# When one weight half is loaded for GpSimd, and which PSUM bank the 256-token groups use, in a fused attention and expert-routing kernel

## The chip, the cores and the metric

The kernel runs on one core of a Trainium2 chip. The metric is the time on the device for one execution, in microseconds (us). Lower is better. Matrix products run on TensorE (PE in the profile), elementwise work on VectorE (DVE), ScalarE (ACT) and GpSimd (POOL). Transfers are issued in order by a queue of SyncE (SP) and, for some, by GpSimd. SBUF is the on-chip memory of 128 partitions; PSUM holds the results of products, in banks of 512 float32 per partition; DRAM lies outside.

## What is computed

The reference first computes an attention without softmax, then a layer of eight experts with Sinkhorn weights. All is float32.

```
# attention: batch 4, heads 4, 1088 tokens, head size 32, r = 8
phi(x): a = S1 x, b = S2 x; outer product of a and b, 64 features
kv  = sum over tokens of phi(k) v^T;   z = sum over tokens of phi(k)
out = (phi(q) kv) / (phi(q) z + 1e-6)
x   = out as (4352 tokens, 128)

# experts: D = 128, E = 8, F = 1024
P = exp(x w_gate - max)
8 times: P /= rows' sums; P /= columns' sums; P *= N / E
out = sum over e of P[:, e] * (relu(x w1[e]) w2[e])
```

## The kernel before

**Stages.** The work runs in three overlapping stages. The attention takes the batches 0 to 3 one after the other (`attention(b)`), then `routing()` computes the logits and eight Sinkhorn rounds. The tokens' features end in `xT` (128 features by 4352 tokens). Since TensorE would often wait during these two stages, `fill(n)` lets it do expert products there that need no routing weights: `steps()` is a generator of such work, one step per call, and the numbers that `attention` and `routing` yield say how many steps' worth go between two of their parts. After that comes the long weighted stage (from about 213 us on), where the other experts' products are computed with tokens already multiplied by their routing weight.

**The groups.** `steps()` walks through 13 groups in the order of the list `groups` (line 672). Each has an expert, a first token and a number n of tokens. Groups 0, 1, 3, 5, 6 and 8 belong to expert 0. Groups 2, 4, 7, 9, 10, 11 and 12 are "SMALL": the first 256 tokens with the experts 1, 2, 4, 3, 5, 6 and 7. A small group has two blocks of four steps. An expert-0 group has four blocks, and works on two sets of n tokens at once. In each step TensorE computes one hidden chunk (`first`, line 787), ScalarE applies Relu to it (line 789), and TensorE issues second products that belong to hidden chunks of eight steps earlier (`LAG = 8`, `into`, line 851).

**Two kinds of second products.** The small groups and group 0 add up plain products (`eight`) in one or two banks of PSUM. The other groups use Strassen-like combinations with seven products instead of eight (`seven`). VectorE forms the differences that they need (line 802), and the products add up in four banks: bank 0 holds p1 and p6, bank 1 p2 and p4, bank 2 p3 and p5, bank 3 p7. In each block they are issued in this order.

**Emptying the banks.** When the last product of a bank is done, `into` calls `part`. For a small group that is one ScalarE copy to `kept_small` (line 699). For a group with seven products it is `part_of_seven`: three copies for bank 0 (lines 723, 724, 726), one for bank 1 (730), three for bank 2 (734 to 736) and two for bank 3 (739, 740). ScalarE works in order, and its Relus stand between these copies. The banks are tiles of the pool `mps` with the tags `s0` to `s3`, one buffer each: whoever takes a tag next waits until the copies out of it are done. In `into` a small group's tag is its expert's number modulo 4. So the groups 2, 4, 7, 9 and 10 use the banks 1, 2, 0, 3 and 1. Groups 11 and 12 are put off and use other lines (866).

**Weights for the small groups.** Expert 1's weights lie in `wb`, in columns 3F to 5F (F = 1024). Expert 2's take the same place: `small_load(2, ...)` is called within `steps()` at the third block of group 3 and issues two transfers on SyncE's queue (lines 1007 and 1010, 512 KB each). Experts 3 to 7 are loaded in `routing()` by `small_weights()`; expert 4's go to `xfs[0]` (called `xf0`).

**Packing on GpSimd.** For the weighted stage, weights are turned into the combinations that the seven products need. Three of these halves are formed by GpSimd at the end of the attention: (4, 0) and (5, 0), the first-layer weights of the experts 4 and 5, and (5, 1), the second-layer weights of expert 5. `bench_load(n, where, e, i)` loads a raw half on SyncE's queue: line 230 for a first-layer half, four transfers of 128 KB, and line 235 for a second-layer half. `bench_pack(n)` has GpSimd do four subtractions or additions (line 201) and then store the result to DRAM (line 247, `packed`). Bench 0 holds (4, 0) and lies in `xf0`; bench 1 holds (5, 1) and lies in two tiles named `qx`; bench 2 holds (5, 0) and lies in `xf0` again. The store of a first-layer half reads a part of the raw half as well, so the next load into `xf0` has to wait until that store is done.

**What orders the queues.** TensorE, VectorE and ScalarE run in the written order during these stages (`manual_schedule`). SyncE's and GpSimd's transfers and GpSimd's arithmetic keep program order too. An instruction at the head of a queue that waits holds up all behind it. In `attention(2)` the order is: the raw halves of bench 0 and bench 1 are asked for; later `take_over(2, ...)` has GpSimd store the finished attention output (`xd`, line 510) and bring it back turned into `xT` (four transfers of line 512), then GpSimd packs bench 0, and bench 2 is loaded. In `attention(3)` `take_over` is issued in two parts: columns 0 to 192 by GpSimd, columns 192 to 288 by SyncE. `logits` (line 520) reads `xT` of all batches. At the start of `routing()` GpSimd packs bench 2 and then bench 1; then the pools of the attention are closed and `first_weights` and `raw_second` load the weights for the weighted stage (`w1f`, `w2r`).

Of the kernel before, what the change touches and what calls it, by code (L numbers as in the profile page):

```python
# [53 lines left out]
def kernel(  # L54
# [38 lines left out]
    xfs = [big.tile([P, 8, 256], F32, name="xf0"),  # L93
           *(wb[:, 2 * F * i:2 * F * (i + 1)].rearrange("p (c n) -> p c n", c=8) for i in range(2))]
# [154 lines left out]
    def raw_half(e, i, raw):  # L249
        if i:  # L250
            load_w2(e, raw.rearrange("p (f d) -> p f d", d=DM))
        else:
            load_w1_halves(e, raw)
# [6 lines left out]
    def halves_in(t):  # L260
        t = t.rearrange("p a n -> p (a n)")[:, 0:32 * H2]
        return t[:, 0:16 * H2], t[:, 16 * H2:], t
# [6 lines left out]
    def bench_load(n, where, e, i):  # L269
        benches[n] = e, i, *where()  # L270
        raw_half(e, i, benches[n][2])
# [47 lines left out]
    def transpose_q(b, lo=0, hi=S):  # L319
        to = kT if b == 1 else qT  # L320
        nc.vector.transpose(out=to[:, lo:hi], in_=loaded["q", b].rearrange("p a d -> p (a d)")[:, lo:hi])
# [38 lines left out]
    def keys_sums(b):  # L360

        kp, vx = products[b], v_slots[b % 2]
        pv = bank()[:, 0:128].rearrange("p (i c d) -> p i c d", i=2, c=2)

        slots = [slice(h, H + 1, H - h) for h in range(H)]

        for t in range(NT + 1):
            n = P if t < NT else 64
            for h in range(H):
                i, s = divmod(h, 2)  # L370
                nc.tensor.matmul(pv[64 * s:64 * (s + 1), i], kp[0:n, H * t + h].rearrange("p i j -> p (i j)"),  # L371
                                 vx[0:n, slots[h], t, :], start=(t == 0 and i == 0), stop=(t == NT and i == 1),
                                 tile_position=(0, 64 * s))
        sums_of[b] = pv
# [3 lines left out]
    def keys_kept(b):  # L378
        pv = sums_of.pop(b)
        for s in range(2):  # L380
            sl = slice(64 * s, 64 * (s + 1))
            if b:
                x, y = kvs[b % 2][sl, :, s, :], pv[sl].rearrange("p i c d -> p i (c d)")[:, :, 0:D + 1]
            else:
                x, y = kvz[sl, :, :, s, :], pv[sl].rearrange("p i c d -> p c i d")
            nc.scalar.copy(x, y)
# [88 lines left out]
    def times(b, c):  # L475
        ph = third(phs[b % 2], c)
        nc.vector.tensor_tensor(ph, ph, third(rb, c), op=Alu.mult)
# [53 lines left out]
    def attention(b):  # L531


        follows = b + 1 < B
        keys_sums(b)
        times(b, 0)
        yield 2.2 if b == 1 else 2
        keys_kept(b)
        times(b, 1)
        tops(b, 0)  # L540
        if b == 1:
            transpose_q(2)
        yield 1.4
        times(b, 2)
        over(b, 0)
        tops(b, 1)
        if b == 1:
            queries_ab(2)
            repeat_a(2)
        if follows:  # L550
            repeat_b(b + 1)
        if b == 2:
            bench_load(0, lambda: halves_in(xfs[0]), 4, 0)
            bench_load(1, halves_in_two, 5, 1)
        yield 1.4
        over(b, 1)
        if b + 1 == B:
            take_over(b, 0, 192, nc.gpsimd)
        yield 1.4
        tops(b, 2)  # L560
        if follows:
            transpose_k(b + 1)
        if b + 2 < B:
            load_k(b + 2)
            load_v(b + 2)
        yield 1.4
        over(b, 2)
        if b + 1 < B:
            take_over(b, 0, W9, nc.gpsimd)
            if b == 2:  # L570
                bench_pack(0)
                bench_load(2, lambda: halves_in(xfs[0]), 5, 0)
        else:
            take_over(b, 192, W9, nc.sync)
        if follows:
            yield 0.7
            keys_ab(b + 1)
            yield 0.7
            if b == 1:
                transpose_q(3)  # L580
            keys_products(b + 1, 0)
            yield 1.4
            keys_products(b + 1, 1)
            if b == 1:
                queries_ab(3)
                repeat_a(3)
            yield 1.4
            keys_products(b + 1, 2)
            yield 1.4
# [10 lines left out]

    def routing():

        for n in (2, 1):
            bench_pack(n)
        early.close()
        pools.append(ctx.enter_context(tc.tile_pool(name="late", bufs=2)))
        for i in range(3):
            first_weights(i)
            raw_second(i)
        small_weights()  # L610
        yield 5
        for c in range(len(chunks)):
            logits(c)
        yield 1
        for c in range(len(chunks)):
            logits_turned()
        lg = lgp[:, :, 0:E]
        mx = sk.tile([P, 1], F32, tag="mx", name="mx")
        nc.vector.tensor_reduce(out=mx, in_=lg, axis=AX.XY, op=Alu.max)
        yield 3  # L620
        pm = bank()[:, 0:P]
        for s in range(2):
            nc.tensor.matmul(pm[64 * s:64 * (s + 1)], mx.to_broadcast([P, 64]), ident, start=True, stop=True,
                             tile_position=(0, 64 * s))
        nc.vector.reduce_max(mx, pm, axis=AX.X)
        nc.vector.tensor_scalar(mx, mx, -1.0, 64 * math.log(2.0), op0=Alu.mult, op1=Alu.add)
        pw = p2s[0]
        nc.scalar.activation(out=pw[:, :, 0:E], in_=lg, func=Act.Exp, bias=mx[:, 0:1])

        step = 1.5 * 2.0 ** (23 - 149 + 64)  # L630
        nc.vector.tensor_scalar(pw[:, :, 0:E], pw[:, :, 0:E], step, step, op0=Alu.add, op1=Alu.subtract)
        for it in range(ITERS):
            rs = sk.tile([P, SA], F32, tag="rs", name="rs")
            nc.vector.reduce_sum(rs, pw, axis=AX.X)
            nc.vector.reciprocal(rs, rs)
            p1 = p1s[it % 2]
            nc.vector.scalar_tensor_tensor(p1[:, 0:SA], rs.unsqueeze(2).to_broadcast([P, SA, E]), UP,
                                           pw[:, :, 0:E], op0=Alu.mult, op1=Alu.mult)
            cs = sk.tile([P, E], F32, tag="cs", name="cs")
            nc.vector.reduce_sum(cs, p1.rearrange("p g e -> p e g"), axis=AX.X)  # L640
            yield 4.25
            pc = bank()[:, 0:E]
            for s in range(2):
                nc.tensor.matmul(pc[64 * s:64 * (s + 1)], ones[:, 0:64], cs, start=True, stop=True,
                                 tile_position=(0, 64 * s))
            cr = sk.tile([P, E], F32, tag="cr", name="cr")
            nc.vector.reciprocal(cr, pc)
            last = it == ITERS - 1
            pw = lgp if last else p2s[(it + 1) % 2]
            nc.vector.scalar_tensor_tensor(pw[:, :, 0:E], cr.unsqueeze(1).to_broadcast([P, SA, E]),  # L650
                                           float(N) / E * (1.0 if last else UP), p1[:, 0:SA],
                                           op0=Alu.mult, op1=Alu.mult)

        nc.vector.transpose(out=lgT.rearrange("p a s -> p (a s)"), in_=lgp.rearrange("p a e -> p (a e)"))
        for b in range(B):
            nc.sync.dma_start(out=pT[:, b * S:(b + 1) * S],
                                                  in_=lgT[32 * b:32 * b + E].rearrange("p a s -> p (a s)"))
# [16 lines left out]
    SMALL = {g for g, group in enumerate(groups) if group[2][0]}  # L674
    DIRECT = {0, *SMALL}
# [3 lines left out]
    items = [(g, e) for g, group in enumerate(groups) for e in group[2]]  # L679
# [160 lines left out]
    def into(g, w, x, i, s):  # L840

        n = groups[g][1]
        if g not in sums:
            banks = (items[g][1] % 4,) if g in SMALL else range(2) if g in DIRECT else range(4)
            sums[g] = [mps.tile([P, 512], F32, tag=f"s{i % 4}", name="s")[:, 0:n] for i in banks]
            done[g] = {}

        seen = done[g]
        c = seen[i, s] = seen.get((i, s), 0) + 1
        per = FO if g in DIRECT else FO // 4 if i == 3 else FO // 2  # L850
        nc.tensor.matmul(sums[g][i][H2 * s:H2 * (s + 1)], w, x, start=c == 1, stop=c == per, tile_position=(0, H2 * s))  # L851
        if c == per:
            seen[i] = seen.get(i, 0) + 1
            if seen[i] == 2:
                part(g, i)
# [585 lines left out]
```

## Time and profile before

| quantity | us |
|---|---|
| median of 3 runs | 917.51 |
| lowest and highest of the 3 | 917.27, 919.56 |
| the profiled execution | 920.07 |
| its span, from the first to the last instruction | 918.1 |

The profile comes from one execution. TensorE's clock is granted by a throttle; its mean over the span was 0.996 of full speed. In lines of the profile, `L787` is line 787 of the kernel, `a<-xT,wb` is what an instruction writes and reads by the program's names, and `x4` a count. `[8.13 <-DMA wb<-...]` says how long the engine was idle before, and what ended the wait. Times are in us from the start of the span. Matmuls are pipelined, so a matmul's end in the records can overlap the next one's start; each float32 product appears as two records, and a pair of products, one for each half of the columns, as four.

### The profile page before, as it was taken

Reading aid. Unit: us, or ns where it says so; the run is one execution under the profiler, and the core shown is the slowest. Engines: PE = TensorE matmul, PEld = TensorE weight load, DVE = VectorE, ACT = ScalarE, POOL = GpSimd, SP = SyncE. Lnnn points to the kernel's source line nnn. Section 1 sums busy time; section 2 is a strip of 40 time slices with the busy share of each in tenths; the row PEclk is TensorE's granted clock in tenths of the full one; section 3 lists DMA queues with packets and bytes.
Section 4 is the critical chain, followed back from the end, with each engine's and each line's share of the span. In section 5 each row is a group of like instructions: output and inputs, shape, how many; then the busy total and the mean of one; then the engine's idle time right before and its main releaser. Section 6 shows DMA issues by size and latency. Waiting matters only on the chain.

```text
span 918.1 us, 34646 instructions
## 1 busy us (share of the span) xinstructions
PE 896.4 (98%) x14664; PEld 715.6 (78%) x14664; DVE 739.9 (81%) x1160; ACT 526.5 (57%) x1276; POOL 357.9 (39%) x381
## 2 busy tenths in 40 slices
PE   8999699999999999999999999999999999999997
PEld 6786357667888677778787777888887899998885
DVE  7667378875999888889879888978889788878974
ACT  3353245556565665666556666656665666566652
POOL 3013400031444434554675553435334443554330
PEclk9999899999999999999999999999999999999999
DMA  8986583033667767777776777767676777767740
GB/s 253 308 268 214 206 255 130 3 114 133 180 215 244 227 191 215 221 232 229 215 206 194 225 216 229 216 195 224 193 214 207 223 224 209 220 206 216 203 127 13
DMA packets 150234, 183.97 MB, mean 200 GB/s; under 512 B 16352, under 2 KB 112368, under 8 KB 149696
## 3 DMA queue, kind: packets, MB, share of 16 engines
q1 hardware_dynamic: 143856, 164.17, 60.4%
q0 software_dynamic: 5024, 17.42, 5.5%
q8 instruction: 116, 1.90, 0.8%
q14 instruction: 38, 0.31, 0.1%
q10 hardware_dynamic: 1200, 0.16, 0.1%
HBM read 148.38 MB, written 18.65 MB: 182 GB/s over the span
## 4 chain that ended last, share of the span: by engine, by line
PE 91%; DMA 2%; issue 2%; DVE 2%; ACT 1%; POOL 1%; SPq 0%; ACTq 0%; POOLq 0%; DVEq 0%
PE s L1136 37%; PE a L1086 36%; PE a L787 8%; PE s L851 6%; DMA xd<-xt 1%; PE s L866 1%; PE a L371 1%; DMA qx<-in_q_dram 1%; DMA wb<-in_moe_w_dram 1%; PE a L1237 0%; DMA packed<-xf 0%; PE s L400 0%; DVE hb L1118 0%; POOL xf L201 0%; PE a L450 0%
## 5 line engine op out<-in xcount | busy, mean ns | idle before, releaser
L1086 PE MATMUL a<-wb,w1f 64*64 64x256 f32 x4144 | 433.1, 377 | 0.2 <-DVE ht L1107 0.2
L1086 PEld LDWEIGHTS a<-wb,w1f 64*64 64x64 f32 x4144 | 275.8, 133 | 35.7 <-DVE ht L1107 2.5
L1086 PE MATMUL a<-xf,w1f 64*64 64x256 f32 x2128 | 230.3, 377 | 0.1
L1100 ACT COPY a<-a 128x256 f32<-128x256 f32 x224 | 80.0, 357 | 216.8 <-PE a L1086 216.7
L1136 PE MATMUL s<-ht,w2r 64*64 64x256 f32 x1344 | 192.2, 377 | 0.0
L1136 PE MATMUL s<-hb,w2r 64*64 64x256 f32 x1344 | 191.1, 377 | 0.0
L201 POOL TENSOR_TENSOR wb<-wb 128x256 f32<-128x256 f32 (+1 forms) x115 | 127.9, 1113 | 113.9 <-DMA wb<-wb 82.5
L1136 PE MATMUL s<-ht,w2f 64*64 64x256 f32 x1216 | 161.0, 377 | 1.9 <-issue 1.2
L1136 PE MATMUL s<-hb,w2f 64*64 64x256 f32 x1216 | 157.6, 376 | 0.0
L1086 PEld LDWEIGHTS a<-xf,w1f 64*64 64x64 f32 x2128 | 142.2, 133 | 18.5 <-issue 1.8
L1136 PEld LDWEIGHTS s<-ht,w2r 64*64 64x64 f32 x1344 | 114.8, 133 | 19.4 <-DVE ht L1121 0.7
L1136 PEld LDWEIGHTS s<-hb,w2r 64*64 64x64 f32 x1344 | 113.6, 133 | 19.3 <-DVE hb L1121 0.6
L789 ACT ACTIVATE hb<-a 128x256 f32<-128x256 f32 (+3 forms) x152 | 66.5, 441 | 87.4 <-PE a L787 84.1
L787 PE MATMUL a<-xT,wb 128*64 128x416 f32 (+3 forms) x448 | 101.8, 463 | 8.1 <-DMA wb<-in_moe_w_dram 8.1
L1136 PEld LDWEIGHTS s<-ht,w2f 64*64 64x64 f32 x1216 | 100.4, 133 | 11.0 <-issue 1.7
L1136 PEld LDWEIGHTS s<-hb,w2f 64*64 64x64 f32 x1216 | 99.0, 133 | 8.1
L851 PE MATMUL s<-hb,wb 128*64 128x416 f32 (+3 forms) x408 | 99.0, 457 | 0.6 <-ACT f L736 0.6
L201 POOL TENSOR_TENSOR xf<-xf 128x256 f32<-128x256 f32 (+1 forms) x62 | 68.4, 1105 | 63.6 <-DMA xf<-xf 47.6
L1107 DVE TENSOR_TENSOR ht<-a,mid 128x256 f32<-128x256 f32 x112 | 47.1, 420 | 50.0 <-ACT a L1095 38.8
L201 POOL TENSOR_TENSOR wb<-wb,xT 128x512 f32<-128x512 f32 x37 | 49.3, 1334 | 96.4 <-DMA wb<-pT 61.2
L1107 DVE TENSOR_TENSOR hb<-a,mid 128x256 f32<-128x256 f32 x112 | 47.1, 421 | 48.2 <-ACT a L1095 41.7
L1095 ACT COPY a<-a 128x256 f32<-128x256 f32 x224 | 80.0, 357 | 9.7 <-PE a L1086 1.0
(203 smaller groups left out, 1679.9 us busy)
## 6 DMA issues: line engine op xcount, KB each, us to landing
w1f<-packed SPq DMA_DIRECT2D x204, 224.0 KB, 5.1
w2r<-in_moe_w_dram SPq DMA_DIRECT2D x56, 512.0 KB, 7.0
w2f<-packed SPq DMA_DIRECT2D x68, 256.0 KB, 4.7
wb<-pT SPq DMA_DIRECT2D x45, 256.0 KB, 4.4
wb<-wb SPq DMA_DIRECT2D x74, 128.0 KB, 4.3
hb<-packed SPq DMA_DIRECT2D x32, 256.0 KB, 6.5
xf<-pT SPq DMA_DIRECT2D x19, 256.0 KB, 4.3
xf<-xf SPq DMA_DIRECT2D x36, 128.0 KB, 4.3
```

The costliest lines, as they stand in the source:

```text
L201: tc.keep_in_program_order(nc.gpsimd.tensor_tensor(*args, op=op))
L371: nc.tensor.matmul(pv[64 * s:64 * (s + 1), i], kp[0:n, H * t + h].rearrange("p i j -> p (i j)"), vx[0:n, slots[h], t, :], start=(t == 0 an ...
L787: nc.tensor.matmul(ph[sl], loaded_w[items[j][1]][0][:, P * f + H2 * s:P * f + H2 * (s + 1)], xT[:, lo:hi], start=True, stop=True, tile_pos ...
L789: nc.scalar.activation(out=out, in_=ph, func=Act.Relu)
L851: nc.tensor.matmul(sums[g][i][H2 * s:H2 * (s + 1)], w, x, start=c == 1, stop=c == per, tile_position=(0, H2 * s))
L866: nc.tensor.matmul(held_banks[i][r][rows[s]], w[rows[r], H2 * s:H2 * (s + 1)], x[rows[r]], start=n // 2 % FO == 0, stop=True, tile_positio ...
L1086: nc.tensor.matmul(half_of(r, b, c, n)[rows[s]], w1s[i][rows[r], 1 + form, u, H2 * s:H2 * (s + 1)], xf(i, x)[rows[r]], start=m == opens, s ...
L1095: nc.scalar.copy(b, a)
L1100: nc.scalar.copy(d, a)
L1107: nc.vector.tensor_tensor(h[:, H3, r], d, m5s[k, r], op=Alu.add)
L1136: nc.tensor.matmul(place[rows[s]], w[form][rows[r], pair, u], h[rows[r], x, pair], start=task in (0, 4) and k in firsts, stop=True, tile_p ...
```

## The change

Two edits. The load of bench 2 moves from the end of `attention(2)` to the start of `routing()`, and there bench 1 is packed ahead of bench 2. In the order of SyncE's queue the four transfers of line 230 then stand behind expert 2's weights and behind the last `take_over`, instead of ahead of both. The bank of a small group is no longer its expert's number modulo 4: it is 1 when the group before it is small too, otherwise 0. So the groups 2, 4, 7, 9 and 10 use the banks 0, 0, 0, 0 and 1. What is computed stays the same.

```diff
@@ -569,7 +569,6 @@
             take_over(b, 0, W9, nc.gpsimd)
             if b == 2:
                 bench_pack(0)
-                bench_load(2, lambda: halves_in(xfs[0]), 5, 0)
         else:
             take_over(b, 192, W9, nc.sync)
         if follows:
@@ -600,7 +599,8 @@
 
     def routing():
 
-        for n in (2, 1):
+        bench_load(2, lambda: halves_in(xfs[0]), 5, 0)
+        for n in (1, 2):
             bench_pack(n)
         early.close()
         pools.append(ctx.enter_context(tc.tile_pool(name="late", bufs=2)))
@@ -841,7 +841,7 @@
 
         n = groups[g][1]
         if g not in sums:
-            banks = (items[g][1] % 4,) if g in SMALL else range(2) if g in DIRECT else range(4)
+            banks = (int(items[g - 1][0] in SMALL),) if g in SMALL else range(2) if g in DIRECT else range(4)
             sums[g] = [mps.tile([P, 512], F32, tag=f"s{i % 4}", name="s")[:, 0:n] for i in banks]
             done[g] = {}
 
```

## The prediction

> **What bounds the kernel now.** I read the page's busy times first, then the list of TensorE's waits, then the timeline of each engine around the longest of them.
>
> ```profile
> span 918.1 us, 34646 instructions
> ...
> PE 896.4 (98%) x14664; PEld 715.6 (78%) x14664; DVE 739.9 (81%) x1160; ACT 526.5 (57%) x1276; POOL 357.9 (39%) x381
> ```
>
> TensorE is busy for 896.4 of 918.1 us. So the end moves only if its 21.7 idle us shrink, if its matmuls run at a better clock, or if it gets new waits. The waits, each as total, number and longest in us:
>
> ```profile
> PE a L787 <- DMA wb<-in_moe_w_dram: 8.1, 1, 8.1
> PE s L851 <- ACT w L740: 2.1, 1, 2.1
> ...
> PE s L851 <- ACT f L736: 0.6, 1, 0.6
> ```
>
> One wait is 8.1 us: the first product of group 4 (expert 2, 256 tokens) waits for expert 2's weights. The next two stand at line 851, where a product waits until ScalarE has emptied its bank. The timeline of SyncE's queue shows why the weights are late (start, length, line, transfer):
>
> ```profile
> 75.14 0.59 SPq L235 DMA_DIRECT2D qx<-in_moe_w_dram  x1
> 94.85 2.38 SPq L230 DMA_DIRECT2D xf<-in_moe_w_dram  x4
> 97.29 0.58 SPq L1007 DMA_DIRECT2D wb<-in_moe_w_dram  x1
> ...
> 113.80 0.60 SPq L510 DMA_DIRECT2D xd<-xt  x1
> 116.27 1.76 SPq L512 DMA_DIRECT2D xT<-xd  x4
> ...
> 131.81 2.11 SPq L1007 DMA_DIRECT2D xf<-in_moe_w_dram  x1
> ```
>
> The queue stands still from 75.73 (75.14 + 0.59) to 94.85. The four transfers at 94.85 are the raw half of expert 5 (line 230), which overwrites the half of expert 4 in `xf0`. They wait for GpSimd and for its store to DRAM. Expert 2's weights (L1007, then L1010) are queued behind. GpSimd's timeline and the chain that ended last:
>
> ```profile
> 84.21 2.18 POOL L512 DMA_DIRECT2D xT<-xd  x4 [7.83 <-DMA xd<-xt]
> 86.41 4.29 POOL L201 TENSOR_TENSOR xf<-xf 128x256 f32<-128x256 f32 x4
> ...
> 96.88 0.73 POOL L510 DMA_DIRECT2D xd<-xt  x1 [5.31 <-DVE xt L505]
> 102.06 2.21 POOL L512 DMA_DIRECT2D xT<-xd  x4 [4.45 <-DMA xd<-xt]
> 104.29 2.92 POOL L201 TENSOR_TENSOR xf<-xf 128x256 f32<-128x256 f32 x4
> ```
> ```profile
> 91.00 3.80 DMA packed<-xf
> 97.29 4.81 DMA wb<-in_moe_w_dram
> ```
>
> GpSimd forms the half at 86.41, the store ends at 94.80, the raw half is asked for, and only then expert 2, which lands 4.81 us after 97.29.
>
> **The change, first part: the moved load.** In the instruction order of the changed kernel SyncE has L1007 and L1010 right behind the `qx` load; the four transfers of line 230 stand behind the last L512, ahead of the `w1f` loads. What lets the two transfers go? They overwrite expert 1's weights in `wb`:
>
> ```profile
> 77.72 0.66 PE L851 MATMUL s<-hb,wb 128*64 128x256 f32 x4
> ...
> 93.24 0.86 PE L851 MATMUL s<-hb,wb 128*64 128x416 f32 x2
> 102.23 1.12 PE L787 MATMUL a<-xT,wb 128*64 128x256 f32 x4 [8.13 <-DMA wb<-in_moe_w_dram]
> ```
>
> The last product with expert 1 ends at 78.38 (77.72 + 0.66). From there a landing takes between 4.81 us (the chain's row) and some 8 us (the 7.83 us that GpSimd idled for an `xd` store in the crowded time before 84.21), so the weights are there between 83 and 87. TensorE wants them at 94.10 (102.23 - 8.13). All of the 8.13 us goes: 8.13. The stall also costs clock (columns: stretch, length, busy time of PE, PEld, DVE, ACT, POOL, granted TensorE clock, DMA share, GB/s):
>
> ```profile
> 102.23:104.49 2.26, 2.26 (x8) 1.10 (x10) 0.00 (x0) 0.38 (x1) 2.25 (x5) 0.50 0.81 217
> 104.49:105.86 1.37, 1.37 (x10) 0.76 (x8) 0.00 (x0) 0.38 (x1) 1.29 (x3) 0.83 0.48 137
> 105.86:107.00 1.14, 1.14 (x11) 0.63 (x9) 0.00 (x0) 0.39 (x1) 1.14 (x2) 1.00 0.00 0
> ```
>
> These are three like steps (one product pair of 256 tokens, one of 416). They take 2.26, 1.37 and 1.14 us at a granted clock of 0.50, 0.83 and 1.00. Without the idle time the first two should run as the third: (2.26 - 1.14) + (1.37 - 1.14) = 1.35 (I keep 1.1 as its low end, since steps overlap). So TensorE is 9.5 us earlier from there on, and with it everything that waits for it.
>
> Expert 2's megabyte now moves beside batch 2's `xd` store, for which GpSimd waits until 84.21. At the 4.81 us of the chain's row that store could land up to some 5 us later, and GpSimd's forming with it. The 5.31 us that GpSimd idles before 96.88 cover that; without this cover the logits below would be late by the rest.
>
> The load that was moved issues four transfers (2.38 us of the queue) at about 109, after L512; the `w1f` loads behind them come 2.4 us later in the order, hidden: expert 4's weights, which are queued after them at 131.81, would be asked for at about 131.8 - 9.5 + 2.4 = 124.7. GpSimd packs expert 5's second-layer half (`qx`) first and the moved half after it. The moved half lands at about 114, is formed by 118 (4.29 us at worst) and stored by 122, and expert 4's load into the same `xf0` may go at 124.7. Cover there is ample: TensorE first uses it at 157.18 (147 after), below.
>
> **Second part: the banks.** Groups 2, 4 and 9 get bank 0 in place of 1, 2 and 3; 7 and 10 keep 0 and 1. ScalarE empties a seven-product group's banks in the order 0, 1, 2, 3:
>
> ```profile
> 191.12 0.48 ACT L726 COPY x<-s 128x384 f32<-128x384 f32 x1
> ...
> 194.77 0.47 ACT L740 COPY w<-s 64x384 f32<-64x384 f32 x1
> ...
> 195.30 0.65 PE L851 MATMUL s<-hb,ht 128*64 128x256 f32 x4 [2.11 <-ACT w L740]
> ```
>
> Bank 0 is empty at 191.60, bank 3 at 195.24, and group 9 wanted its bank at 193.19 (195.30 - 2.11). All 2.11 us go. ScalarE has a backlog of copies here, and the first products behind need its Relu to free one of four other banks. Were TensorE to run into that, I reckon with half coming back (low end 1.0); four banks are some four steps of cover, so I take 2.11. Group 4's 0.6 goes the same way.
>
> New waits: behind groups 2 and 4 the next group's first product now needs bank 0 one step after its last use. Group 7 shows the price, since it has bank 0 already:
>
> ```profile
> 174.66 0.87 PE L787 MATMUL a<-xT,wb 128*64 128x384 f32 x4
> 175.38 0.87 PE L851 MATMUL s<-hb,wb 128*64 128x384 f32 x4
> 176.07 0.81 PE L787 MATMUL a<-xT,wb 128*64 128x384 f32 x4
> 176.72 0.81 PE L851 MATMUL s<-hb,wb 128*64 128x384 f32 x4
> ```
>
> From first to second product it is 0.72 us there, and 0.65 one step on. So 2 x 0.07 = 0.15 lost (bounds 0 and 0.4, one copy of 0.37 us: the row of 78.47 below).
>
> **What is late next.** The logits (line 520) need the last third of the attention output: VectorE divides, SyncE stores `xd`, and four L512 transfers bring it into `xT`.
>
> ```profile
> 111.83 0.59 DVE L717 TENSOR_TENSOR z<-x,z 128x416 f32<-128x416 f32 x1 [14.15 <-ACT x L726]
> ```
> ```profile
> wb<-in_moe_w_dram SPq DMA_DIRECT2D x4, 512.0 KB, 7.0
> ...
> xT<-xd SPq DMA_DIRECT2D x4, 48.0 KB, 2.0
> ```
> ```profile
> 119.32 2.37 PE L520 MATMUL a<-xT,wg 128*32 128x512 f32 x24
> 78.47 0.37 ACT L699 COPY kept<-s 128x256 f32<-128x256 f32 x1
> 157.18 0.81 PE L787 MATMUL a<-xT,xf 128*64 128x256 f32 x4
> ```
>
> (The second fence gives the median us from issue to landing.) Four L512 are issued in 1.76 us, the last near 117.6, and it lands 2.0 later, at 119.6. TensorE begins the logits at 119.32 and wants the fourth batch after three of twelve products, some 0.6 us on (a quarter of 2.37, an estimate). That leaves a slack of 0.3 us. The chain starts from TensorE, so it moves with the 9.5 us, but not with group 4's 0.6, which falls between its start and its end. I count that 0.6 as given back. VectorE's part may also grow: it stood idle for 14.15 us before 111.83, and most of GpSimd's packing from 104.29 on fell into that. Now the `qx` pack begins when GpSimd's L512 ends, between 102 and 104, and VectorE's add and divide begin at 102.3. What overlap costs:
>
> ```profile
> 79.41 2.27 DVE L802 TENSOR_TENSOR hb<-hb 128x832 f32<-128x832 f32 x3
> 86.46 3.66 DVE L802 TENSOR_TENSOR hb<-hb 128x832 f32<-128x832 f32 x3 [3.59 <-PE s L851]
> ```
>
> Three like differences take 2.27 us alone and 3.66 beside GpSimd's forming, a factor of 1.6. VectorE's add and divide last from 111.83 to L510 at 113.80, 1.97 us; at 1.6 they lose 1.2, with no overlap 0, with all four pack steps ahead 2.9 (the 2.92 of 104.29). I take half of 1.2: 0.6. [...]
>
> **Sum.** 8.13 + 1.35 + 2.11 + 0.6 - 0.6 - 0.15 - 0.6 = 10.84 us less. The profiled execution took 920.07 us (span 918.1 and 1.97 around it), so 909.2 under the profiler. The median of the plain runs is 917.51, which is 2.56 less, and I take the same difference from it: 906.7. Its own range: best, nothing is given back (8.13 + 1.35 + 2.11 + 0.6 = 12.19), 905.3; worst, 8.13 + 1.1 + 1.0 - 0.4 - 2.9 = 6.9, 910.6.
>
> **Rivals.** *The logits chain becomes the bound.* Beside the 2.9 us of the pack, the `xd` store may share the DMA engines with the `packed` store of `qx`: it then takes the 4.45 us that GpSimd idled at 102.06 in place of 1.87 (113.80 + 0.60 to 116.27). Together 2.9 + 2.6 = 5.5 in place of 0.6: 911.6. For it: the small slack. Against: the pack ends after 105, so its store comes behind the `xd` store, which is due at 104.3.
>
> *The change doesn't do what it says:* expert 2's weights still come late, since 1 MB more meets the crowded time around 76 to 84. Then only the banks count, 2.11 + 0.6 - 0.15 = 2.56: 915.0. Against: 7 us of slack.
>
> *Slower:* SyncE serves in order, and expert 4's load now waits for the store of the moved half. Behind it stand the loads for experts 6 and 7 and the stores of the routing weights. Issued after 139.4 (157.18 less 10.8 less a landing of 7.0), each us of lateness is a us of TensorE time; issued after 150.2 the kernel is slower than before, at 154 by 3.8 us: 921.3. For it: the margin between 122 and 124.7 is thin. Against: nearly 15 us follow before it costs anything, and GpSimd does nothing else then (the span in 40 slices of 23 us, busy tenths; slices 6 to 8 are 115 to 184 us):
>
> ```profile
> POOL 3013400031444434554675553435334443554330
> ```
>
> **How the numbers follow.** Forecast 0.75, logits 0.14, not as it says 0.06, slower 0.05. A measurement of this kernel tells some 0.3% (2.75 us) from no change: 914.8 to 920.3. Forecast and logits are faster: 0.89. The third case lies inside the bound: 0.06. Slower 0.05. The range, 904.9 to 911.2, holds the forecast's own and nearly all of the logits case; its low end leaves another 0.4 us for the scatter of the runs.
>
> **What would show it.** L1007 issued near 76 and L1010 near 79 on SyncE; no wait of line 787 for `wb`, and a granted clock of 1.00 from 94 to 107; no wait of line 851 for L740 or L736, and 0.1 us or less for L699 behind groups 2 and 4; a wait of line 520 for `xT` of about 1 us. Line 230 issued near 109 and expert 4's load near 125. It is wrong if line 787 waits again, now for `xf` (expert 4), if line 520 waits over 3 us, or if the steps after 94 stay slow.

## The result, and the profile after

| quantity | before, us | after, us |
|---|---|---|
| median of 4 runs each | 917.39 | 905.25 |
| lowest and highest | 916.06, 919.56 | 902.61, 906.62 |
| the profiled execution | 920.07 | 902.61 |
| its span | 918.1 | 900.6 |

The ratio is 0.9862, with an interval of 0.9832 to 0.9892: faster by 12.7 us on 917.51 (9.9 to 15.4), where 10.8 were forecast. In a second comparison the ratio is 0.9849 (0.9827 to 0.9870). The two profiled executions differ by 17.5 us; section by section below, that is more than the change is worth.

The busy times of the changed kernel's page:

```profile
span 900.6 us, 34646 instructions
...
PE 891.1 (99%) x14664; PEld 718.5 (80%) x14664; DVE 739.4 (82%) x1160; ACT 526.2 (58%) x1276; POOL 361.4 (40%) x381
```

TensorE's idle time fell from 21.7 to 9.5 us. Its waits, from the list of waits (total, number, longest):

```profile
PE s L1136 <- DVE hb L1048: 1.1, 1, 1.1
PE a L119 <- POOL own L121: 1.0, 1, 1.0
PE a L338 <- DVE mid L326: 0.8, 1, 0.8
PE a L416 <- ACT kvz L386: 0.6, 1, 0.6
PE a L520 <- DMA xT<-xd: 0.4, 1, 0.4
...
```

Line 787's 8.1 us for `wb` and line 851's 2.1 and 0.6 us are gone. One wait is new, that of the logits for `xT`. SyncE's queue:

```profile
74.63 0.59 SPq L235 DMA_DIRECT2D qx<-in_moe_w_dram  x1
75.31 0.53 SPq L1007 DMA_DIRECT2D wb<-in_moe_w_dram  x1
77.74 1.03 SPq L1010 DMA_DIRECT2D wb<-in_moe_w_dram  x1
102.77 0.60 SPq L510 DMA_DIRECT2D xd<-xt  x1
105.28 1.91 SPq L512 DMA_DIRECT2D xT<-xd  x4
107.29 2.64 SPq L230 DMA_DIRECT2D xf<-in_moe_w_dram  x4
...
125.81 2.10 SPq L1007 DMA_DIRECT2D xf<-in_moe_w_dram  x1
```

Expert 2's weights are asked for at 75.31 instead of 97.29; the moved half at 107.29 and expert 4's weights at 125.81 stand where the prediction put them (near 109 and 125). TensorE's timeline around the old stall, then around the logits:

```profile
91.32 0.92 PE L787 MATMUL a<-xT,wb 128*64 128x416 f32 x4
92.05 0.51 PE L851 MATMUL s<-hb,wb 128*64 128x416 f32 x1
92.08 0.59 PE L787 MATMUL a<-xT,wb 128*64 128x256 f32 x2
...
107.65 1.06 PE L520 MATMUL a<-xT,wg 128*32 128x512 f32 x6
109.16 1.99 PE L520 MATMUL a<-xT,wg 128*32 128x512 f32 x18 [0.45 <-DMA xT<-xd]
111.08 0.92 PE L787 MATMUL a<-xT,wb 128*64 128x416 f32 x4
...
115.94 0.39 PE L623 MATMUL a<-ident,mx 128*64 128x128 f32 x4
```

Group 4's first product starts 0.76 us behind the last 416-token one (92.08 - 91.32), where it was 9.75 before (102.23 - 92.48). The windows show the steps that were slow before (length, busy time of each engine, granted clock, DMA share, GB/s):

```profile
92.08:93.21 1.13, 1.13 (x11) 0.88 (x9) 0.65 (x2) 0.52 (x1) 0.00 (x0) 1.00 0.87 362
93.21:94.34 1.13, 1.13 (x11) 0.88 (x9) 1.10 (x3) 0.38 (x1) 0.00 (x0) 1.00 0.00 0
```

Each takes 1.13 us at a clock of 1.00, instead of 2.26 and 1.37. The weighted stage begins with line 866:

```profile
L866 PE MATMUL s<-hb,wb x128: 373/376/427, 200.0 to 214.2; 64*64 64x256 f32 x128
```

It begins at 200.0 instead of 212.8, 12.8 us earlier, and from there to the end of the span the two executions take 700.6 and 705.3 us.

### The profile page after: what moved, and what is told of

Its sections match the earlier page's. It is cut to its first block, busy times and chain, and to the rows that moved or that the text cites. A ratio compares the mean times of both kernels' runs of the same rounds, so it can differ in the third digit from the quotient of the medians.

```text
span 900.6 us, 34646 instructions
## 1 busy us (share of the span) xinstructions
PE 891.1 (99%) x14664; PEld 718.5 (80%) x14664; DVE 739.4 (82%) x1160; ACT 526.2 (58%) x1276; POOL 361.4 (40%) x381
## 4 chain that ended last, share of the span: by engine, by line
PE 96%; DVE 2%; DMA 1%; ACT 0%; SPq 0%; issue 0%; ACTq 0%; DVEq 0%
PE a L1086 37%; PE s L1136 37%; PE a L787 9%; PE s L851 8%; PE a L371 1%; PE s L866 1%; PE a L486 1%; DMA qx<-in_q_dram 1%; PE a L1237 0%; PE s L400 0%; PE a L450 0%; PE a L338 0%; DMA xd<-xt 0%; DMA xT<-xd 0%; PE s L416 0%
## 5 line engine op out<-in xcount | busy, mean ns | idle before, releaser
L201 POOL TENSOR_TENSOR wb<-wb,xT 128x512 f32<-128x512 f32 x37 | 52.1, 1410 | 92.7 <-DMA wb<-pT 62.9
L1098 ACT COPY mid<-a 128x256 f32<-128x256 f32 x224 | 84.7, 378 | 0.0
```

The source lines that it names most:

```text
L201: tc.keep_in_program_order(nc.gpsimd.tensor_tensor(*args, op=op))
L1098: nc.scalar.copy(m5s[k, r], c)
```

## The experiments

**Each edit alone, and the other place for the moved half.** `load_only` keeps the old line for the banks; `banks_only` is the kernel before with the new one. `other_place` takes the wait away in another way: the raw half stays where it was in the queue but goes to free memory, so that it waits for no store.

```diff
 load_only, from the kernel after
-            banks = (int(items[g - 1][0] in SMALL),) if g in SMALL else range(2) if g in DIRECT else range(4)
+            banks = (items[g][1] % 4,) if g in SMALL else range(2) if g in DIRECT else range(4)
 other_place, from the kernel before with the new banks
-                bench_load(2, lambda: halves_in(xfs[0]), 5, 0)
+                bench_load(2, lambda: halves_in(kept[:, N - 32 * H2:].rearrange("p (a n) -> p a n", a=8)), 5, 0)
```

> The first edit alone: the moved load and the swapped packing order, with the old banks. Theory A (the wait for expert 2 costs from start to start: its first product would have begun beside the last product ahead of it, at 93.24 of the trace of before, so 8.99 us and not the 8.13 idle us of the records; and 1.35 for the slow clock): group 4's first product starts near 92.1, as in the changed kernel; the wait of line 851 for L736 (0.6 us) and for L740 (2.1 us) are back; time about 10 us less than before, 907 to 908. Theory B (the idle us of the records are the whole price, the rest of the measured change lies in the weighted stage): 8.13 + 1.35 - 0.5 = 9.0 less, 908.4, and the weighted stage, from the first product of line 866 to the end, is shorter than before's by some us again.

> The second edit alone: the new banks with the load at its old place. Both theories: the 8.1 us wait of line 787 stays, followed by steps at a granted clock of 0.50 and 0.83; the waits of line 851 for L736 and L740 are gone. 2.1 us less than before, and up to 0.6 more for group 4 if the logits do not give it back: 914.7 to 915.3. If the bank of group 9 only moves its wait to the first products behind ScalarE's backlog, it is 1 us or less: 916.4 or more.

> The new banks; the raw half of expert 5 is asked for at its old position in SyncE's queue and packed in the old order, but lies in columns of the tile kept that no group has written yet, so that its load has nothing to wait for. Theory A (the price is SyncE's queue standing still behind a waiting load, not where the load stands): L1010 is issued before 82, group 4's first product does not wait, time as the changed kernel within 0.5 us, 904.7 to 905.8. Rival (half a megabyte more ahead of expert 2's weights in the crowded time makes them or batch 2's features late): a wait of line 787 of 1 us or more, 906.5 or more.

| kernel | median, us | ratio | interval |
|---|---|---|---|
| `load_only` | 906.63 | 0.9885 | 0.9865 to 0.9904 |
| `banks_only` | 914.92 | 0.9972 | 0.9957 to 0.9988 |
| `other_place` | 904.74 | 0.9868 | 0.9848 to 0.9889 |

Both edits pay, and they add up: 1.15% + 0.28% = 1.43%, and both together gave 1.38% and 1.51%. By its time alone `load_only` doesn't tell its two theories apart: it is 10.6 us below the 917.86 us of the old kernel measured beside it, with an interval of 8.8 to 12.4, and they gave about 10 and 9.0. The traces below do. `other_place` issued L1010 at 84.60, later than the 82 that was expected, but has no wait of line 787 and the time of the changed kernel: the gain comes from expert 2's weights no longer standing behind a waiting load, wherever that load is put.

TensorE's timeline in `banks_only`, where the stall is left, and the windows behind it:

```profile
92.53 0.93 PE L787 MATMUL a<-xT,wb 128*64 128x416 f32 x4
...
103.70 1.12 PE L787 MATMUL a<-xT,wb 128*64 128x256 f32 x4 [9.58 <-DMA wb<-in_moe_w_dram]
...
121.31 3.16 PE L520 MATMUL a<-xT,wg 128*32 128x512 f32 x24
124.40 0.92 PE L787 MATMUL a<-xT,wb 128*64 128x416 f32 x4
```
```profile
103.70:105.96 2.26, 2.26 (x8) 1.10 (x10) 0.00 (x0) 0.38 (x1) 2.18 (x4) 0.50 0.88 248
105.96:108.20 2.24, 2.24 (x10) 1.08 (x8) 0.00 (x0) 0.38 (x1) 1.84 (x4) 0.50 0.37 154
```

The same stall is 9.58 us long here, not 8.13, and two steps behind it run at half clock, not one. In `load_only`, where group 9's bank is left as it was, the wait stands and clock is lost behind it:

```profile
185.19 0.69 PE L851 MATMUL s<-hb,ht 128*64 128x256 f32 x4 [2.12 <-ACT w L740]
185.67 1.06 PE L787 MATMUL a<-xT,ht 128*64 128x256 f32 x4
```
```profile
186.00:188.00 2.00, 2.00 (x12) 1.18 (x10) 2.00 (x1) 0.39 (x1) 2.00 (x3) 0.50 0.98 341
```

**The clock by itself.** Nine products whose result is not read stand ahead of group 4's first product in the kernel before, so that TensorE is busy while it waits.

```diff
+                if g == 4 and q == 0:
+                    busy = bank()
+                    for _ in range(9):
+                        nc.tensor.matmul(busy, ones, xT[:, 0:512], start=True, stop=True)
```

> The kernel before with nine more products of 128x512, whose result nobody reads, on TensorE ahead of group 4's first product (about 7.7 us of work where TensorE idled 8.1 us). Theory A (the slow steps behind the stall come from the clock, which falls when TensorE idles): the granted clock stays 1.00 from 93 to 107, the first step of group 4 takes 1.1 us instead of 2.26, the second 1.1 instead of 1.37, and the time is 1.35 us less than before, 916.0. Rival (these steps are slow because ScalarE or the weights are late): they stay slow, and the time is before's or more.

Measured: 916.73 us, ratio 0.9990 (0.9977 to 1.0004); by time alone this can't be told from nothing. TensorE's timeline and the windows behind the stall show the mechanism:

```profile
92.78 7.99 PE L903 MATMUL a<-xT,ones 128*128 128x512 f32 x18
100.91 0.65 PE L787 MATMUL a<-xT,wb 128*64 128x256 f32 x4
```
```profile
100.91:102.06 1.15, 1.15 (x8) 0.71 (x10) 0.00 (x0) 0.38 (x1) 1.15 (x3) 1.00 0.94 275
102.06:103.19 1.13, 1.13 (x10) 0.69 (x8) 0.00 (x0) 0.38 (x1) 1.11 (x3) 1.00 0.70 170
```

Behind a stall filled with products the first steps take 1.15 and 1.13 us at a clock of 1.00. From group 4's first product to the logits (line 520, at 116.66) it is 15.75 us here, where the two traces of the kernel before have 17.09 and 17.44. All 12 runs have a mean granted clock of 0.998 or more; the 23 runs of the kernel before beside them have 0.991 to 0.996. So the slow steps follow from TensorE's idleness, not from late weights: the first step ran at a clock of 0.50 behind 8.13, 9.58 and 10.02 idle us (the traces of the kernel before, `banks_only` and `before_again`), and at 1.00 behind 7.99 us of products.

**The changed kernel and the old one once more.** The same two kernels, and `load_only`, were run again to see how far single traces scatter.

> The changed kernel once more, on the chip and beside the same runs of before as the three others of this call. Both theories: 905.3 within 1 us. From the first product of line 866 to the end 700 to 701 us, as in every execution but the profiled one of before (705.3); if the change itself shortened the weighted stage, this kernel's differs from that of the kernels without the change in the same way again.

> The kernel before once more, for a second trace of its stall. Theory A (the price of a wait is counted from start to start and has a clock part that varies from execution to execution): the time from the last 416-token first product ahead of group 4 (near 92.5) to group 4's first product is its idle time plus 1.6 us again, where the changed kernel needs 0.76; the steps behind it lose 1.3 to 2.7 us to the clock; from the first product of line 866 to the end it is 700 to 705 us. Theory B (the weighted stage is longer without the change): 705 us again, beside 700.6 and 703.9 for the changed kernel.

> The first edit alone once more. In its first trace the 2.1 us wait for L740 was followed by three steps at a granted clock of 0.50 to 0.87, which cost 1.8 us more; in the trace of before the same wait was followed by a clock of 1.00. Theory A (whether a wait of that length costs clock changes from execution to execution): from the first product of line 623 to that of line 866 it is 86.3 us (no clock lost) or 88.1 (lost), and 84.1 in every kernel with the new banks. Rival (the moved load itself makes the steps behind that wait slow): 88.1 again.

`after_again` took 904.83 us, `before_again` 920.7 and `load_only_again` 906.45 (one run each for the last two). The old kernel's second trace, TensorE and then windows:

```profile
92.28 0.93 PE L787 MATMUL a<-xT,wb 128*64 128x416 f32 x4
...
103.89 1.12 PE L787 MATMUL a<-xT,wb 128*64 128x256 f32 x4 [10.02 <-DMA wb<-in_moe_w_dram]
```
```profile
103.89:106.15 2.26, 2.26 (x8) 1.08 (x10) 0.00 (x0) 0.39 (x1) 1.96 (x4) 0.50 0.90 227
106.15:107.86 1.71, 1.71 (x10) 0.95 (x8) 0.00 (x0) 0.38 (x1) 1.61 (x3) 0.66 0.48 202
```

The stall is 10.02 us long in this execution. So the profiled execution from which the prediction was made had the shortest of the three stalls that were traced (8.13, 9.58, 10.02). Cut at the same instructions, the four traces of the two kernels give (us; a timeline can merge the first record of group 4 into the row of the 416-token product ahead, as in `after_again`, where the record itself starts at 93.02):

| stretch | before | again | after | again | less by | predicted |
|---|---|---|---|---|---|---|
| from the start to the last 416-token product ahead of group 4 | 92.48 | 92.28 | 91.32 | 92.30 | 1.2, 0.0 | 0 |
| on to group 4's first product | 9.75 | 11.61 | 0.76 | 0.73 | 9.0, 10.9 | 8.13 |
| on to the logits (line 520) | 17.09 | 17.44 | 15.57 | 15.64 | 1.5, 1.8 | 1.35 + 0.6 - 0.15 |
| on to line 623 | 7.14 | 6.94 | 8.29 | 8.37 | -1.2, -1.4 | -0.6 - 0.6 |
| on to line 866 | 86.3 | 86.3 | 84.0 | 84.0 | 2.3, 2.3 | 2.11 |
| on to the end | 705.3 | 704.1 | 700.6 | 703.9 | 4.7, 0.2 | 0 |

In the last stretch, which the change doesn't touch, the fourteen traces of this study lie between 700.2 and 705.3 us. The kernel before has the two longest, but the changed kernel's second is close to them, and `banks_only` and `warm_stall`, with the load at its old place, have 701.0 and 700.8: 4.7 of the 17.5 us between the first two spans are put down to scatter. That speaks against theory B of `load_only`, which had the change itself shorten this stretch. In `load_only_again` group 9's wait was followed by no slow step, unlike in `load_only`:

```profile
186.22 0.65 PE L851 MATMUL s<-hb,ht 128*64 128x256 f32 x4 [2.12 <-ACT w L740]
```
```profile
186.00:188.00 2.00, 1.78 (x17) 1.21 (x19) 1.80 (x1) 0.93 (x3) 2.00 (x3) 1.00 1.03 430
```

**What holds up the logits.** Three kernels ask it. `qx_early` lets GpSimd pack `qx` in `attention(2)`, so that no packing runs beside VectorE's division. `old_pack_order` packs the moved half first and `qx` behind it, which also makes that store as late as it can be for expert 4's weights. `logits_later` was to give the chain more time.

```diff
 qx_early, from the kernel after: in attention(2), then in routing
                 bench_pack(0)
+                bench_pack(1)
-        for n in (1, 2):
-            bench_pack(n)
+        bench_pack(2)
 old_pack_order, from the kernel after
-        for n in (1, 2):
+        for n in (2, 1):
 logits_later, from the kernel after
-        yield 5
+        yield 5.6
-        yield 3
+        yield 2.4
```

> The changed kernel with expert 5's second-layer half packed right behind expert 4's first half, ahead of batch 3's transfers on GpSimd, so that GpSimd neither computes nor stores while VectorE divides and the last third comes into xT. Theory A (the logits are late because their chain has no slack once the banks are faster; VectorE's steps took 1.95 us in the changed kernel, as before): their wait stays within 0.3 us of 0.45 us, or falls by the half us that the store beside the transfers may cost; time within 0.6 us of the changed kernel. Rival, the prediction's (GpSimd's packing slows VectorE's divide by 0.6 us, and with it the logits): the wait goes, 0.6 us or more less. In both cases TensorE may wait longer at line 486 near 91, since GpSimd now works beside VectorE's products there.

> The changed kernel with the old order of packing: the moved half first and expert 5's second-layer half after it. The store of the latter then lands near 122.6 instead of 108.5, the first w1f load, which takes the place of the tile qx, waits for it in SyncE's queue (from 110.2), and expert 4's first-layer weights are issued near 138 and land near 145, where TensorE wants them at 146. Theory A (what stands behind a waiting load costs nothing until TensorE has come to it): no wait of line 787, time within 0.5 us of the changed kernel, or at most 1 us more if the landing takes longer than 7 us. Rival of the prediction (lateness in this queue turns into TensorE time at once): the 12 us show in large part, 910 or more.

> The changed kernel with the logits one step of expert work later (0.6 more is yielded ahead of them, 0.6 less between the largest logit and its spread to all partitions). Theory A (in the changed kernel the logits are where TensorE meets the transfers into xT, and give back what the banks gain there, about 1.1 us): no wait of line 520, 7.1 to 7.5 us instead of 8.3 from the first product of line 520 to that of line 623 less the step moved out, and about 1 us less in all, 904.2. Rival (the wait comes back behind, since the routing then starts later and TensorE waits at line 623 or 644): no gain, 905 or more.

Measured: 904.75 (0.9857, 0.9838 to 0.9876), 904.49 (0.9852, 0.9833 to 0.9871) and 904.54 us (0.9855, 0.9836 to 0.9873). By time none can be told from the changed kernel. `logits_later` failed as an experiment: the numbers round to the same steps, and TensorE's order came out unchanged, so its trace is one more of the changed kernel's order. VectorE and GpSimd in the kernel after, then VectorE's last step before:

```profile
100.80 0.59 DVE L717 TENSOR_TENSOR z<-x,z 128x416 f32<-128x416 f32 x1 [4.31 <-ACT x L726]
101.31 0.23 DVE L499 RECIPROCAL rc<-a 128x12 f32<-128x12 f32 x1
101.57 0.56 DVE L501 TENSOR_TENSOR rd<-a,rc 128x384 f32<-128x384 f32 x1
102.17 0.58 DVE L505 STREAM_TRANSPOSE xt<-rd 128x384 f32<-128x384 f32 x1
102.67 1.00 DVE L717 TENSOR_TENSOR kept<-x,m 64x416 f32<-64x416 f32 x1
```
```profile
101.67 3.29 POOL L201 TENSOR_TENSOR qx<-qx 128x256 f32<-128x256 f32 x4
105.26 0.58 POOL L247 DMA_DIRECT2D packed<-qx  x1 [0.30 <-POOL qx L201]
```
```profile
113.70 0.54 DVE L717 TENSOR_TENSOR kept<-x,m 64x416 f32<-64x416 f32 x1
```

GpSimd packs from 101.67 to 104.96, over the division (L501) and the transpose (L505), and these take 0.56 and 0.58 us, as before. Add to store is 1.97 us again (102.77 - 100.80): VectorE loses nothing on the chain. The next step, a sum with two inputs from SBUF, takes 1.00 us where the same step took 0.54 before. So beside GpSimd's packing this sum ran 0.46 us longer, and the division and the transpose no longer than before; what sets them apart is shown by no run. In `qx_early` GpSimd packs nothing there, and the wait is no shorter (SyncE, then TensorE):

```profile
105.34 0.61 SPq L510 DMA_DIRECT2D xd<-xt  x1
```
```profile
111.84 1.99 PE L520 MATMUL a<-xT,wg 128*32 128x512 f32 x18 [0.56 <-DMA xT<-xd]
```

But `qx_early` moves something else as well: the earlier packing makes GpSimd's own part of `take_over` late (its four L512 start at 104.48, in the kernel after at 99.43), and these now run beside SyncE's `xd` store. So the transfers have to be looked at in two parts. The six traces in which the logits visibly wait give (us; starts in each trace):

| trace | `xd` store (L510) | first L512 of SyncE | GpSimd's next `packed` store | logits go on | from L510 to L512 | from L512 on |
|---|---|---|---|---|---|---|
| `after` | 102.77 | 105.28 | 105.26 | 109.16 | 2.51 | 3.88 |
| `after_again` | 103.78 | 106.29 | 106.24 | 110.25 | 2.51 | 3.96 |
| `logits_step_place` (below) | 104.29 | 106.76 | 106.83 | 112.38 | 2.47 | 5.62 |
| `logits_later` | 103.50 | 106.27 | 107.94 | 109.76 | 2.77 | 3.49 |
| `other_place` | 105.23 | 108.18 | 109.88 | 111.81 | 2.95 | 3.63 |
| `qx_early` | 105.34 | 108.43 | 118.60 | 111.84 | 3.09 | 3.41 |

Where GpSimd's store of a packed half is issued within 0.1 us of the first L512, the second part takes 3.88 us or more, elsewhere 3.41 to 3.63. In the last three traces GpSimd is still issuing its own four L512 when the `xd` store goes out (until 103.76, 105.61 and 106.69), and there the first part is longer. This is read from traces that differ in several things; no run isolates it.

`old_pack_order` tries the slower rival. Its queue:

```profile
108.60 2.40 SPq L230 DMA_DIRECT2D xf<-in_moe_w_dram  x4
123.47 2.38 SPq L230 DMA_DIRECT2D w1f<-in_moe_w_dram  x4
...
137.50 2.06 SPq L1007 DMA_DIRECT2D xf<-in_moe_w_dram  x1
```
```profile
147.70 0.71 PE L787 MATMUL a<-xT,xf 128*64 128x256 f32 x3
```

The queue stands from 111.0 (108.60 + 2.40) to 123.47, and expert 4's weights are asked for at 137.50, 11.7 us later than in the kernel after. TensorE takes them at 147.70 with no wait ahead. That is still short of the 139.4 from which the prediction counted lateness as TensorE time, so a load later than that was not tried. Neither packing nor a `packed` store stands beside SyncE's L512 here (GpSimd's packing starts at 113.24), and the logits have no idle wait.

**One step more ahead of the logits.** The same aim as `logits_later`, with whole steps, and once more with the raw half in its old place (the edit of `other_place`).

```diff
 logits_step, from the kernel after
-        yield 5
+        yield 6
-        yield 3
+        yield 2
```

> The changed kernel with the logits one step of expert work later: 6 is yielded ahead of them and 2 in place of 3 behind them, and TensorE's order differs by that one step alone. Theory A (the logits are where TensorE meets the transfers into xT): no wait of line 520; from the third step behind group 4's first product to the first product of line 623 about 0.5 to 1.1 us less than in the changed kernel; time 904 to 904.8. Rival (the wait comes back at line 623, which has one step less in front): 905 or more.

> The same as logits_step, and the raw half is asked for at its old position into unused columns of the tile kept, as in other_place. Theory A: as logits_step within 0.5 us, since neither the load's place in the queue nor GpSimd's order is on TensorE's path any more. Rival: the load ahead of expert 2's weights delays batch 2's and 3's features and with them the logits: 1 us or more slower than logits_step.

Measured: 904.34 us (0.9846, 0.9820 to 0.9873) and 905.27 us (0.9855, 0.9827 to 0.9883). TensorE in `logits_step`:

```profile
109.06 2.46 PE L520 MATMUL a<-xT,wg 128*32 128x512 f32 x24
...
115.19 0.39 PE L623 MATMUL a<-ident,mx 128*64 128x128 f32 x4
```

The logits run through without a wait, and line 623 follows group 4's first product (its first record starts at 92.31) 22.9 us later, where the traces of the changed kernel have 23.9 (115.94 - 92.08) and 24.0. That 1 us can't be told from nothing in the time: 904.34 against 904.83. `logits_step_place` missed its expectation of 0.5 us around `logits_step`: its median is 0.9 us higher, and the logits wait again, for 1.02 us. No version is clearly faster than the changed kernel.

## Why the prediction came out as it did

*Right: the place and the mechanism.* The queue stood behind a load that waited for a store; expert 2's weights now go ahead, and the stall and its slow steps are gone in every trace of the new order.

*The step that failed: "All of the 8.13 us goes: 8.13".* The term was sized too small. Measured from start to start, this stretch became 9.0 us shorter in the first pair of traces and 10.9 in the second. Two things are in that. An idle record counts from the end of the last work, but group 4's first product starts 0.76 us behind the previous one's start, beside its second products, when nothing holds it: the stretch is 0.86 us longer than the idle time in the first pair (9.75 - 0.76 - 8.13). And the stall has no fixed length, since it ends with a chain of GpSimd, a store, a load and another load: 8.13, 9.58 and 10.02 us in three traces, and the prediction's was the shortest. The other terms, 2.71 us by the prediction, add up to 2.7 us in both pairs. With this stretch that makes 11.7 and 13.6 us, on both sides of the measured 12.1 and 13.3 (the two comparisons' medians), so the shortfall lies in this term. That the stalls of the untraced runs are longer than 8.13 us too is inferred. By the ratio the median came out just under the range's low end (904.85 against 904.9): both ends of the range keep 8.13 as it is. The top, 911.2, is also below the 911.6 of the logits rival, so it doesn't hold nearly all of that case, as the prediction says.

*The clock, 1.35: right, with scatter.* The two steps behind the stall cost 1.35 us in the first trace, 1.70 in `before_again` ((2.26 - 1.14) + (1.71 - 1.13)) and 2.24 in `banks_only` ((2.26 - 1.13) + (2.24 - 1.13)), where a third window was slow as well (2.37 us at a clock of 0.81). The profiled execution was a mild one: its mean granted clock of 0.996 is the highest in the 41 runs of the kernel before that stand beside these experiments (0.991 to 0.996). `warm_stall` shows the cause: with TensorE kept busy the two steps took 1.15 and 1.13 us.

*Group 9's bank, 2.11: right.* The stretch to line 866 is 2.3 us shorter, and 84.0 to 84.1 us in all kernels with the new banks; no wait appeared behind it, and none of line 851 for the new bank 0 behind groups 2 and 4 (0.15 in the sum). In `load_only`, where the wait stands, clock was lost on top of it (the stretch took 88.1 us there and 86.4 in `load_only_again`), a price the prediction didn't count.

*Group 4's 0.6, given back at the logits: right.* From group 4's first record (92.33) to the logits (108.57) `load_only` needs 16.24 us, the kernel after 15.57, so 0.7 us is gained there. In `banks_only` the logits' products fill 3.09 us (124.40 - 121.31), where they fill 2.30 before (121.62 - 119.32): 0.8 given back.

*VectorE's 0.6: right in size, wrong in cause.* In the kernel after the logits fill 3.43 us (111.08 - 107.65), 1.13 more than before, against 1.2 for both terms; the row's 0.45 is only the part of it that shows as idle time. But VectorE lost nothing: from add to store it took 1.97 us again. What is left beside the banks' 0.8 is the transfers: from the store's issue to the continued logits it takes 6.39 us (109.16 - 102.77), where before 6.1 were enough (119.32, a quarter of 2.37 more, less 113.80). The traces point to GpSimd's store of the packed `qx`: it was issued at 105.26, beside the L512 of 105.28. The prediction had this store in its logits rival, beside the `xd` store, and set it aside because it would come behind that one. It did come behind it, and met the transfers that follow. That it is the cause is not shown by a run of its own.

*Expert 2's transfers beside batch 2's store.* Up to 5 us were feared; GpSimd waits 7.13 us for that store in the kernel after and 7.83 before. Nothing was lost.

*The rivals.* The logits did not become the bound: 1.1 us given back, not 5.5. "Doesn't do what it says" fell with the vanished wait. The slower rival fell with the trace of the changed kernel: expert 4's weights were asked for at 125.81, 13.6 us ahead of the 139.4 from which it would have cost anything. In `old_pack_order` they were asked for 11.7 us later still, and TensorE waited for nothing.

## What to carry to other kernels

Price a stall from start to start of the same two instructions, with and without it, not by its idle record; add the slow steps behind it (1.35 to 2.24 us here); and where it ends with a chain of transfers, take its length from more than one execution. In a queue that works in order, look for the load that waits for a store, and for what stands behind it: moving it was worth 1.15%, and the list of waits names only the transfer that came last. When two spans are compared, cut them at the same instructions first: here a quarter of the difference (4.7 of 17.5 us) lay in a stage that the change never touched.

## What the runs showed of the hardware

The same wait of 2.12 us before the same product was followed by a clock of 1.00 in `load_only_again` and of 0.50 in `load_only`, where that stretch took 1.7 us more. That the wait alone is the cause is not shown. Behind the long stall the loss was 1.35, 1.7 and over 2.2 us for stalls of 8.13, 10.02 and 9.58 us, so it doesn't follow the stall's length. And the weighted stage, the same instructions each time, took between 700.2 and 705.3 us from one execution to the next. Of the 4.7 us between the first two traces, 1.7 are TensorE's waits (lines 1136 and 1086: 3.1 us in all before, 1.4 after); what moves the rest stays open.
